# Units 0 to 2 of a chunked-attention and MLP kernel, written out as one list of instructions

## The chip, the cores and the metric

The kernel runs on one core of a Trainium2 chip. The metric is device microseconds of one execution; before the change the median of three runs is 231.96 us (231.26 to 234.47). The core has five engines that run their own instruction queues in order: PE (matmul; PEld is its weight load), DVE, ACT, POOL and SP. Transfers are issued from POOL's queue when they cast, and from SP's or ACT's queue when they don't; all of them share 16 DMA engines.

## What is computed

Attention over chunks of 32 queries, with 16 keys of left context, 8 of right context and 8 memory keys, then a LayerNorm and a two-layer MLP with a residual, over 4 batches of 768 tokens, 8 heads of 64:

```python
for c in range(nc):                                  # nc = 768 // 32
    k_full = concatenate([mem_k, k[:, :, l_start:r_end]], axis=2)
    v_full = concatenate([mem_v, v[:, :, l_start:r_end]], axis=2)
    a = softmax(0.125 * q_c @ k_full.T)
    out[:, :, c_start:c_end] = a @ v_full
x = out.transpose(0, 2, 1, 3).reshape(B, S, 512)
xn = (x - mean(x)) / sqrt(var(x) + 1e-6) * g_ln
y = x + maximum(xn @ w_ch1, 0) @ w_ch2               # 512 -> 2048 -> 512
```

All inputs and the output are 32 bit in memory. The kernel computes in 16 bit with 32-bit sums.

## The kernel before

**Tiles and units.** A tile t (0 to 23) is 128 tokens, six tiles to a batch. A unit u (0 to 11) is two tiles, 256 tokens, the width of an MLP matmul. The attention of a tile runs some units ahead of its MLP.

**Attention of a tile.** `qk_products` (line 305) multiplies the transposed queries QD with the key stream KT, in which the memory keys are repeated in front of every group of 64 keys (`mem_cols`, 189). `row_max` and `less_max` (324, 327) take the row maximum off on DVE, `weights` (337) is the exponential on ACT, `pt` (344) transposes the weights on PE and copies them to PT. `val_products` (355) multiplies them with V, whose rows are [16 left, 16, memory, 24 shared] and the same for the second half of a group; `tokens` (369) divides by the row sums and takes the mean on DVE, `shift` (382) subtracts the mean on POOL or ACT, `turn_x` (410) transposes to x^T on PE and copies it on DVE, `root` (398) computes 1/sqrt(var+eps) on ACT and POOL.

**K, Q and V into place.** An octet is 8 consecutive tokens, 2 KB per head in memory. `load_octets` (108) casts octets of k, q or v into `raw[0]`, `raw[1]` or `raw[2]`, one load for the even heads and one for the odd (`par`). Batch 0 is loaded in two parts and turned by `turn` (208) on PE: 16 small matmuls for two head pairs, then `to_stream` (223) or `to_rows` (232) copies the result out of PSUM. V of batch 0 is turned twice, through the stream VT (the same tile as KT[1]) by `v_products` (278) and `v_copy` (295). Later batches use `mix` (243), a copy that sets two heads side by side, and `turn_mixed` (251), 8 matmuls instead of 16. V of batches 1 to 3 is loaded straight into place, two loads a head (`load_v_head`, 116) and two for the ends; `v_shared` and `v_mem` (140, 144) then copy rows from SBUF to SBUF through SP's queue.

**MLP of a unit.** `up` (447): eight slots s of 8 matmuls with a quarter of w1 (w1c[s // 2]), then a relu. The gain g is multiplied into w1 beforehand, 16 POOL instructions (`scale_w1`, 425). `down` (473) is the plain second layer and serves unit 0; from unit 1 on `down7` (544) does the same with seven products of 8 matmuls in place of eight, with sums of weights (`w2_sum`, 495) and of activations (`r_sum`, 512) made on DVE. `add_to` (533) multiplies by 1/sqrt(var+eps) and adds to x, `store` (539) writes the tile.

**The order.** The program order is each engine's queue order, and the waits between engines follow from the tiles. Units 0 and 1 are written out by hand (603 to 818) with PSUM banks by turns (`slot`, `use`), and with 32 matmuls on zeros as filler (`warm`, 596). From unit 2 (line 884) a plan places attention, loads and sums between the slots `up(u, s)` and the products `down7(u - 1, part)`. Up to line 818 POOL's queue holds, in this order: k and q of octets 0 to 47 and 0 to 31, the identity, v, w1[0], w1[1], the second parts of k, q, v, scaling and w1[2], scaling and w1[3], w2, the other scaling, k and q of batch 1, V of batch 1 head by head.

Of the kernel before, what the change touches and what calls it, by code (L numbers as in the profile page):

```python
# [16 lines left out]
def kernel(  # L17
# [29 lines left out]
    memKT = sb.tile([128, B * 4, 8], FP16, name="memKT")  # L47
    memVT = sb.tile([128, 4, 8], FP16, name="memVT")
# [8 lines left out]
    memk32 = T[1].bitcast(FP32).rearrange("p n (x c) -> p (n x) c", c=64)[0 : B * H, 0:8, :]  # L57
    memv32 = T[1].bitcast(FP32).rearrange("p n (x c) -> p (n x) c", c=64)[0:H, 8:16, :]
    memk16 = T[0].rearrange("p n (x c) -> p (n x) c", c=64)[0 : B * H, 0:8, :]
    memv0 = T[0].rearrange("p n (x c) -> p (n x) c", c=64)[0:H, 8:16, :]  # L60
# [24 lines left out]
    six = one + upb + dnb  # L85
    banks = {"list": six, "turn": 0}
# [4 lines left out]

    def use(*b):
        banks["list"], banks["turn"] = list(b), -1
# [14 lines left out]
    def load_octets(i, half, src, b, lo, n):  # L108

        for par in range(2):  # L110
            nc.gpsimd.dma_start(  # L111
                out=raw[i][half][par : 2 * n : 2],
                in_=dram(src, (b * H + par) * HS + 512 * lo, [[512, n], [2 * HS, 4], [1, 512]]),
            )
# [24 lines left out]

    def v_shared(b, g0, g1):  # L140
        vt = V[b % 2]
        nc.sync.dma_start(out=vt[40:64, g0:g1, :, :], in_=vt[72:96, g0:g1, :, :])

    def v_mem(b, rows=(32, 64), ng=NG):
        src = memv16[:, b, :, :]
        for lo in rows:
            nc.sync.dma_start(
                out=V[b % 2][lo : lo + 8, 0:ng, :, :],
                in_=bass.AP(tensor=src.tensor, offset=src.offset,
                            ap=[list(src.ap[0]), [0, ng], [1, H * VW]]),  # L150
            )
# [12 lines left out]
    def load_mem(dst, src, n):  # L164
        nc.sync.dma_start(out=dst, in_=dram(src, 0, [[512, n], [1, 512]]))
# [9 lines left out]
    def mem_turn(dst, src, n):  # L175

        p = slot()
        half = n // 2
        for m in range(8):
            for par in range(2):  # L180
                nc.tensor.matmul(
                    out=p[64 * par : 64 * par + 64, half * m : half * m + half],
                    lhsT=src[0:n, m, :],
                    rhs=free(identity[0:n, :], 2 * par, [[4, half // 2], [1, 2]]),
                    start=True, stop=True, tile_position=(0, 64 * par),
                )
        nc.vector.tensor_copy(out=dst, in_=free(p, 0, [[1, half], [half, 8]]))

    def mem_cols(dst, src, ends):
        s = list(src.ap[0])  # L190
        nc.vector.tensor_copy(
            out=free(dst, 32, [[KC, 4], [BLK, NG], [1, 8]]),
            in_=bass.AP(tensor=src.tensor, offset=src.offset, ap=[s, [8, 4], [0, NG], [1, 8]]),
        )
        if ends:
            nc.vector.tensor_copy(
                out=free(dst, 0, [[KC, 4], [8, 2], [1, 8]]),
                in_=bass.AP(tensor=src.tensor, offset=src.offset, ap=[s, [8, 4], [0, 2], [1, 8]]),
            )
            nc.vector.tensor_copy(  # L200
                out=free(dst, KC - 8, [[KC, 4], [1, 8]]),
                in_=bass.AP(tensor=src.tensor, offset=src.offset, ap=[s, [8, 4], [1, 8]]),
            )

    def copy_on(engine):
        return nc.scalar.copy if engine == "A" else nc.vector.tensor_copy
# [25 lines left out]
    def to_rows(b, pv, jj, engine, n, oct0, lo=0, hi=None):  # L232
# [7 lines left out]
    mixed = [raw[2][x].rearrange("p j r d -> p (j r d)").rearrange("p (j r c) -> p j r c", j=2, c=128)  # L240
             for x in range(2)]

    def mix(i, half, engine):

        for jj in range(2):
            copy_on(engine)(
                out=mixed[i][0:96, jj].rearrange("p r (x d) -> p x r d", x=2),
                in_=raw[i][half][0:96, 2 * jj : 2 * jj + 2],
            )

    def turn_mixed(i, jj):

        pv = as16(slot())
        for r in range(8):
            nc.tensor.matmul(  # L255
                out=pv[:, 96 * r : 96 * r + 96],
                lhsT=mixed[i][0:96, jj, r, :], rhs=identity[0:96, 0:96],
                is_transpose=True, start=True, stop=True,
            )
        return pv  # L260

# [6 lines left out]
    def turn_k(b, half, jj, engine):  # L268
        to_stream(KT[b % 2], turn(raw[0][half], jj, 48), jj, engine, 48, 48 * half)

    def turn_q(b, half, jj, engine, p=None):
        n, oct0 = (48, 48 * half) if b else ((64, 32) if half else (32, 0))
        to_rows(b, turn(raw[1][half], jj, n, p), jj, engine, n, oct0)

    def turn_v(half, jj, engine):
        to_stream(VT, turn(raw[2][half], jj, 48), jj, engine, 48, 48 * half)

    def v_products(g):

        p = slot()  # L280
# [18 lines left out]

    def v_turn(g, engine):  # L300
        v_copy(g, v_products(g), engine)


# [40 lines left out]
    def pt(t, engine="A"):  # L344
        p = slot()
        pv = as16(p)[:, 0:512]
        for j in range(4):
# [4 lines left out]
            )  # L352
        copy_on(engine)(out=PT[t % 3].rearrange("p j q -> p (j q)"), in_=pv)  # L353

# [27 lines left out]
    def shift(t, engine="P"):  # L382
        x, i = xs[t % 9], t % 3
        if engine == "P":
            nc.gpsimd.tensor_scalar(  # L385
                out=xn[i], in0=x, scalar1=nmean[t % 6], scalar2=1.0, op0=ALU.add, op1=ALU.mult,
            )
        else:
            nc.scalar.activation(
                out=xn[i], in_=x, func=ACTF.Identity, bias=nmean[t % 6], scale=1.0,  # L390
            )
# [6 lines left out]
    def root(t):  # L398
# [4 lines left out]
        )  # L403
        nc.gpsimd.tensor_scalar(  # L404
# [5 lines left out]
    def turn_x(t, p=None):  # L410
        p = slot() if p is None else p
        pv = as16(p)[:, 0:512]
        for dt in range(4):
# [4 lines left out]
            )  # L418
        i = t % 2
        nc.vector.tensor_copy(  # L420
            out=xT[(t // 2) % 3][:, :, 128 * i : 128 * i + 128],
            in_=pv.rearrange("p (d c) -> p d c", d=4),
        )

    def scale_w1(c, dt, engine):
        w = w1c[c][:, dt, :]
        if engine == "A":
            nc.scalar.activation(out=w, in_=w, func=ACTF.Copy, scale=g_col[:, dt : dt + 1])
        elif engine == "V":
            nc.vector.tensor_scalar(  # L430
                out=w, in0=w, scalar1=g_col[:, dt : dt + 1], scalar2=None, op0=ALU.mult,
            )
        else:
            nc.gpsimd.tensor_scalar(
                out=w, in0=w, scalar1=g_col[:, dt : dt + 1], scalar2=1.0,
                op0=ALU.mult, op1=ALU.mult,
            )


# [7 lines left out]
    def up(u, s, engine="A"):  # L447
        p = upb[s % 2]
        for hb in range(2):
            hc = 2 * s + hb  # L450
            for dt in range(4):
# [5 lines left out]
                )  # L457
        relu(rT[u % 2][:, 2 * s : 2 * s + 2, :], p.rearrange("p (h c) -> p h c", h=2), engine)

    def up_half(s, i, p, engine=None):  # L460
# [9 lines left out]
        if engine:  # L470
            relu(rT[0][:, 2 * s : 2 * s + 2, :], p.rearrange("p (h c) -> p h c", h=2), engine)

    def down(u, part):
        i, quarter = divmod(part, 4) if u else (part % 2, part // 2)
        p, t = dnb[i], 2 * u + i
        for hc in range(4 * quarter, 4 * quarter + 4):
            nc.tensor.matmul(  # L477
                out=p, lhsT=rT[u % 2][:, hc, 128 * i : 128 * i + 128],
# [3 lines left out]
        if quarter == 3:  # L482
            x = xs[t % 9]
            nc.vector.scalar_tensor_tensor(
                out=x, in0=p, scalar=rstd[t % 9], in1=x, op0=ALU.mult, op1=ALU.add,
            )
            nc.sync.dma_start(out=out[t // 6, 128 * (t % 6) : 128 * (t % 6) + 128, :], in_=x)
# [56 lines left out]
    def down7(u, part, tail=False):  # L544
        t, s = 2 * u, 2 * u + 1
# [6 lines left out]


        if part == 0:
            product(dnb[0], r_block(u, 0, 0), block(0, 0), False)
            add_to(t, 0, dnb[0])
        elif part == 1:
            product(dnb[1], r_block(u, 0, 1), block(1, 0), False)
            add_to(t, 0, dnb[1])
        elif part == 2:  # L560
            product(dnb[0], RS[1], total(1), True)
            add_to(t, 1, dnb[0])
        elif part == 3:
            product(dnb[1], RS[0], total(0), False)
            add_to(s, 1, dnb[1])
        elif part == 4:
            product(dnb[0], RS[2], total(2), True)
            add_to(s, 1, dnb[0])
            if tail:
                store(s, 256, 512)  # L570
        elif part == 5:
            product(dnb[1], RS[3], block(1, 1), True)
            add_to(t, 1, dnb[1])
            store(t)
        elif part == 6:
            product(dnb[0], r_block(u, 1, 1), total(3), True)
            add_to(s, 0, dnb[0])
# [18 lines left out]
    def warm(n, p=upb[1]):  # L596
# [5 lines left out]

    load_mem(memk32, mem_k, B * H)
    load_mem(memv32, mem_v, H)
    load_octets(0, 0, k, 0, 0, 48)
    load_octets(1, 0, q, 0, 0, 32)
    make_identity(nc, identity)
    load_octets(2, 0, v, 0, 0, 48)
    load_w1(0)
    load_w1(1)  # L610
    load_octets(0, 1, k, 0, 48, 48)
    load_octets(1, 1, q, 0, 32, 64)
    load_octets(2, 1, v, 0, 48, 48)
    nc.gpsimd.memset(last, 1.0)
# [320 lines left out]
```

## Time and profile before

| | |
|---|---|
| median of three runs | 231.96 us (231.26 to 234.47) |
| the profiled execution | 231.75 us, span 230.0 us |
| granted TensorE clock | 1.000 over the span |
| busy: PE, DVE, ACT, POOL | 218.4, 162.1, 124.6, 115.4 us |
| first matmul with w1 (line 464) | 19.30 us |
| first matmuls of unit 3, `up(3, 0)` | 76.61 us |
| scores of tile 0 (line 316) | 9.28 us |

The span runs from the first to the last instruction; some 1.75 us of an execution lie outside it. "Busy" counts an instruction from its start to the modelled end, so that PE can be busy without being dense: 8 matmuls of 256 columns follow each other at 0.87 to 0.88 us in the chain that ended last. A row of the timeline gives the start, the time taken, engine and line, the operation with its output and input, the number of instructions, and in brackets the idle time before it and what ended it.

### The profile page before, as it was taken

The numbers are of one execution on the slowest core, as the hardware profiler recorded it, in microseconds if no ns is written. First come the engines' busy times: TensorE is split into PE (matmuls) and PEld (weight loads), VectorE is DVE, ScalarE is ACT, GpSimd is POOL, SyncE is SP. The second block draws the span as 40 slices with busy tenths as digits, with TensorE's granted clock in tenths as the row PEclk, the third lists the DMA queues.
The fourth block names the chain that finished last, engine by engine and source line by source line (L and its number), as shares of the span: only waits on it lengthen the run. The fifth ranks groups of instructions, "written<-read, shape, count | busy, mean of one in ns | idle before, by whom it ended". The sixth has DMA issues, their size and how long they took to land.

```text
span 230.0 us, 8554 instructions
## 1 busy us (share of the span) xinstructions
PE 218.4 (95%) x3720; PEld 190.0 (83%) x3720; DVE 162.1 (70%) x380; ACT 124.6 (54%) x237; POOL 115.4 (50%) x197
## 2 busy tenths in 40 slices
PE   7979787999999989999999999999999999999993
PEld 3546675886898979989989999999999999899982
DVE  3576654678998996796587796894784875646372
ACT  2244475888552748649645468478447265343310
POOL 7889897589965594913724946513031121220000
PEclk9999999999999999999999999999999999999999
DMA  5999999998999899963881992942102002011022
GB/s 79 188 205 205 214 215 200 187 77 55 61 155 152 149 90 111 138 87 42 149 115 51 119 154 56 106 91 67 48 3 91 3 3 91 3 48 46 1 94 93
DMA packets 43282, 23.25 MB, mean 101 GB/s; under 512 B 29884, under 2 KB 39676, under 8 KB 43172
## 3 DMA queue, kind: packets, MB, share of 16 engines
q0 software_dynamic: 38320, 14.48, 52.9%
q1 hardware_dynamic: 4924, 8.22, 12.8%
q8 instruction: 29, 0.48, 0.8%
q14 instruction: 9, 0.07, 0.1%
HBM read 29.02 MB, written 6.29 MB: 153 GB/s over the span
## 4 chain that ended last, share of the span: by engine, by line
PE 86%; DVE 6%; issue 3%; ACT 2%; POOL 1%; DVEq 0%; POOLq 0%
PE upb L452 34%; PE dnb L528 28%; PE two L362 4%; PE one L255 3%; PE dnb L477 3%; PE one L316 3%; PE one L414 2%; PE two L599 2%; PE one L348 2%; POOL raw L111 1%; DVE sub L328 1%; DVE xs L372 1%; DVE KT L227 1%; DVE nmx L325 1%; ACT rT L443 1%
## 5 line engine op out<-in xcount | busy, mean ns | idle before, releaser
L452 PE MATMUL upb<-xT,w1c 128*128 128x256 f16 x736 | 94.9, 273 | 1.6 <-issue 1.4
L452 PEld LDWEIGHTS <-w1c 128*128 128x128 f16 x736 | 77.8, 114 | 3.6 <-issue 1.5
L443 ACT ACTIVATE rT<-upb 128x512 f16<-128x512 f32 x92 | 53.5, 594 | 37.8 <-PE upb L452 34.9
L535 DVE SCALAR_TENSOR_TENSOR xs<-dnb,rstd,xs 128x256 f32<-128x256 f32 x77 | 37.0, 481 | 27.2 <-PE dnb L528 26.3
L528 PEld LDWEIGHTS <-RS 128*128 128x128 f16 x352 | 33.8, 98 | 3.7 <-issue 0.2
L338 ACT ACTIVATE P<-sub 128x512 f16<-128x512 f32 x24 | 15.2, 634 | 37.1 <-DVE sub L328 36.8
L528 PE MATMUL dnb<-T,RS 128*128 128x256 f16 x264 | 33.9, 273 | 0.0
L385 POOL TENSOR_SCALAR xn<-xs,nmean 128x512 f16<-128x512 f32 x18 | 12.7, 707 | 35.6 <-PE upb L452 20.6
L404 POOL TENSOR_SCALAR veps<-ssq 128x1 f32<-128x1 f32 x24 | 4.9, 204 | 45.9 <-ACT sq L400 45.6
L528 PEld LDWEIGHTS <-rT 128*128 128x128 f16 x264 | 25.2, 98 | 2.5
L528 PE MATMUL dnb<-w2c,rT 128*128 128x256 f16 x176 | 22.7, 272 | 0.0
L522 DVE TENSOR_TENSOR RS<-rT 128x1024 f16<-128x1024 f16 (+2 forms) x23 | 15.2, 663 | 8.9 <-ACT rT L443 8.9
L120 POOL DMA_DIRECT2D V<-in_v_dram x24 | 20.9, 871 | 1.2 <-PE dnb L528 0.7
L400 ACT ACTIVATE sq<-xs,nmean 128x512 f16<-128x512 f32 x24 | 17.3, 721 | 0.1
L372 DVE CUSTOM_DVE_ANT_1 xs<-two,rec 128x512 f32<-128x512 f32 x24 | 16.6, 691 | 0.8
L325 DVE TENSOR_REDUCE nmx<-one 128x8 f32<-128x512 f32 x22 | 15.1, 685 | 1.2 <-PE one L316 1.2
L408 POOL TENSOR_TENSOR rstd<-veps,mhalf 128x1 f32<-128x1 f32 x24 | 14.9, 621 | 2.0
L328 DVE TENSOR_TENSOR sub<-one,nmx 128x512 f32<-128x512 f32 x22 | 15.2, 692 | 0.8
L125 POOL DMA_DIRECT2D V<-in_v_dram x24 | 15.5, 647 | 0.0
L353 ACT COPY PT<-one 128x512 f16<-128x512 f16 x21 | 12.2, 586 | 5.6 <-PE one L348 5.6
L255 PEld LDWEIGHTS <-raw 96*128 96x128 f16 x192 | 10.6, 97 | 2.0 <-issue 0.8
L420 DVE COPY xT<-one 128x512 f16<-128x512 f16 x21 | 8.8, 420 | 4.5 <-PE one L414 4.1
(115 smaller groups left out, 312.2 us busy)
## 6 DMA issues: line engine op xcount, KB each, us to landing
out_dram<-xs SPq DMA_DIRECT2D x23, 256.0 KB, 2.5
raw<-in_k_dram POOLq DMA_DIRECT2D x16, 192.0 KB, 5.8
raw<-in_q_dram POOLq DMA_DIRECT2D x12, 192.0 KB, 6.3
w1c<-in_moe_w_ch_dram POOLq DMA_DIRECT2D x4, 512.0 KB, 8.8
w2c<-in_moe_w_ch_dram POOLq DMA_DIRECT2D x4, 512.0 KB, 12.5
V<-in_v_dram POOLq DMA_DIRECT2D x24, 77.0 KB, 3.7
V<-V SPq DMA_DIRECT2D x3, 360.0 KB
V<-in_v_dram POOLq DMA_DIRECT2D x24, 44.0 KB, 3.4
```

Source lines behind the costliest of these rows:

```text
L120: nc.gpsimd.dma_start(out=V[b % 2][72:128, 0 : NG - 1, h, 0:64], in_=dram(v, base + 16 * D, [[64, 56], [64 * 64, NG - 1], [1, 64]]),)
L125: nc.gpsimd.dma_start(out=V[b % 2][0:32, 1:NG, h, 0:64], in_=dram(v, base + 48 * D, [[64, 32], [64 * 64, NG - 1], [1, 64]]),)
L255: nc.tensor.matmul(out=pv[:, 96 * r : 96 * r + 96], lhsT=mixed[i][0:96, jj, r, :], rhs=identity[0:96, 0:96], is_transpose=True, start=True ...
L325: nc.vector.tensor_reduce(out=nmx[t % 2], in_=scores, axis=AX.X, op=ALU.max)
L328: nc.vector.tensor_tensor(out=sub[t % 2].rearrange("p (c k) -> p c k", c=8), in0=scores, in1=free(nmx[t % 2], 0, [[1, 8], [0, 64]]), op=AL ...
L338: nc.scalar.activation(out=P[t % 3], in_=sub[t % 2], func=ACTF.Exp, scale=0.125)
L372: nc.vector.tensor_tensor_reduce(out=x.rearrange("p (h d) -> p h d", h=H), in0=free(two, 0, [[128, 8], [1, 64]]), in1=free(r, 0, [[1, 8], ...
L400: nc.scalar.activation(out=sq, in_=xs[t % 9], func=ACTF.Square, bias=nmean[t % 6], scale=1.0, accum_out=ssq[i],)
L443: nc.scalar.activation(out=o, in_=i, func=ACTF.Relu)
L452: nc.tensor.matmul(out=p[:, 256 * hb : 256 * hb + 256], lhsT=free(w1c[hc // 4][:, dt, :], hc % 4, [[4, 128]]), rhs=xT[u % 3][:, dt, :], st ...
L528: nc.tensor.matmul(out=p[:, 0:256], lhsT=left[:, n, :], rhs=right(n), start=(n == 0 and not add), stop=(n == 7), skip_group_check=add,)
L535: nc.vector.scalar_tensor_tensor(out=x, in0=p[:, 0:256], scalar=rstd[t % 9], in1=x, op0=ALU.mult, op1=ALU.add,)
```

## The change

Units 0 to 2 become one list in which every step names its PSUM bank and its engine, and the plan starts at unit 3. Helpers are split, so that a matmul group and its copy can stand apart (`v_products` and `v_copy`, `up_products` and `relu_up`, `square` and `root_of`, `down7_products` and `add_to`). The parts:

- The octets 0 to 15 of k, q and v of batch 0 come as 32 bit through SP's queue into xs[6] to xs[8], are cast by ACT and DVE and turned by `first_turn`. The memory rows and the octets 16 and 48 of k and v come through ACT's queue, are cast and turned together (`mem_products`, one copy).
- The rest of batch 0 comes in octets 16 to 47 and 48 to 95, and is turned as later batches are, by `mix_into` and `turn_whole`; three of these copies and two `mix` are on POOL.
- w1 comes after all of batch 0, in the order 3, 2, 0, 1. V of batch 1 comes by groups of 64 keys, two loads a group. Of batch 2, the octets 0 to 47 are loaded and mixed in the list; V of its heads 0 to 3 is moved from unit 2 to unit 4.
- g is multiplied into x^T in the copy out of PSUM (`x_copy`); `scale_w1` is gone. Filler falls from 32 matmuls to 13.

```diff
+    def load_v_group(b, g, part):
+        if part == 0:
+            rows = 56 if g < NG - 1 else 48
+            nc.gpsimd.dma_start(
+                out=V[b % 2][72 : 72 + rows, g, :, 0:64],
+                in_=dram(v, b * H * HS + (64 * g + 16) * D, [[64, rows], [HS, H], [1, 64]]),
+            )
...
+    def load_first(queue, x, src):
+        queue.dma_start(out=xs[6 + x], in_=dram(src, 0, [[512, 16], [HS, H], [1, 512]]))
...
+    def mix_into(m, r, jj, rows, engine):
+        copy_on(engine)(
+            out=m[0:rows, jj].rearrange("p r (x d) -> p x r d", x=2),
+            in_=r[0:rows, 2 * jj : 2 * jj + 2],
+        )
...
+    def x_copy(t, pv):
-        nc.vector.tensor_copy(
+        nc.vector.tensor_tensor(
             out=xT[(t // 2) % 3][:, :, 128 * i : 128 * i + 128],
-            in_=pv.rearrange("p (d c) -> p d c", d=4),
-        )
+            in0=pv.rearrange("p (d c) -> p d c", d=4),
+            in1=free(g_col, 0, [[1, 4], [0, 128]]), op=ALU.mult,
+        )
...
+    load_first(nc.sync, 0, k)
+    load_first(nc.sync, 1, q)
+    load_first(nc.sync, 2, v)
+    load_mem(nc.scalar, 0, mem_k, B * H)
+    load_two(B * H, k)
...
     make_identity(nc, identity)
+    nc.gpsimd.memset(V[0][:, 0:4, :, 64:VW], 1.0)
...
+    warm(7, upb[0])
+    nc.gpsimd.memset(V[0][:, 4:NG, :, 64:VW], 1.0)
...
+    load_octets(1, 0, q, 0, 16, 32, (1,))
...
+    load_octets(0, 0, k, 0, 16, 32, (1,))
...
+    s0 = qk_products(0, upb[1])
...
+    mix_into(whole[0], raw[2][0], 0, 64, "P")
...
+    load_octets(1, 1, q, 0, 48, 48, (1,))
...
+    load_w1(3)
...
+    load_w1(2)
...
+    load_v_group(1, 5, 1)
+    load_w1(0)
...
+    mix_into(whole[2], raw[2][1], 1, 96, "P")
...
+    load_w1(1)
...
+    mix_into(whole[1], raw[0][1], 0, 96, "P")
...
+    shift(1, "P")
...
+    up_products(0, 5, dnb[1])
...
+    load_v_group(1, 3, 0)
...
+    load_v_group(1, 2, 0)
...
+    load_octets(1, 0, q, 1, 0, 48, (1,))
...
+    load_octets(1, 0, q, 1, 0, 48, (0,))
...
+    load_w2(0)
...
+    load_mem_rows(1, B)
+    load_octets(0, 0, k, 1, 0, 48, (0,))
...
+    load_octets(0, 0, k, 1, 0, 48, (1,))
...
+    load_w2(2)
...
     ready_v(1, nc.gpsimd)
...
+    shift(3, "P")
...
+    load_w2(1)
...
+    load_v_group(1, 1, 1)
...
+    load_v_group(1, 8, 1)
...
+    load_v_group(1, 9, 0)
...
+    load_v_group(1, 4, 0)
...
+    load_w2(3)
...
+    load_octets(0, 1, k, 1, 48, 48, (1,))
...
+    load_octets(0, 1, k, 1, 48, 48, (0,))
+    mix(0, 1, "V")
...
+    mix(1, 1, "P")
+    lq10 = turn_whole(mixed[1], 0, 96, dnb[1])
+    to_rows(1, lq10, 0, "A", 48, 48)
+    lk10 = turn_whole(mixed[0], 0, 96, upb[0])
...
+    mix(0, 0, "P")
...
+    root_of(7)
+    relu_up(2, 5, one[1], "A")
+    store(1)
...
+                    at(4, n, load_v_head, b, n // 2, n % 2)
...
-    for u in range(2, NP):
+    for u in range(3, NP):
```

Between w2[3] and the last k of batch 1 the list has, on POOL's queue: V group 1 (part 0), k, group 0 (part 0), q, group 10 (part 1), q, groups 6 and 0 (part 1), group 11 (part 0), k. From the turn `lk10` to the end PE's queue holds 7 `up_products`, 7 `down7_products`, 3 `turn_whole`, 2 `val_products`, 2 `qk_products` and 2 `x_products`. After it, unit 3 begins with `up(3, 0)` and then turns `mixed[0]`, which `mix(0, 0, "P")` has written.

## The prediction

> **What bounds the kernel now.** I read the page first, then tables of busy time by stretch, then the timeline.
>
> ```profile
> span 230.0 us, 8554 instructions
> ...
> PE 218.4 (95%) x3720; PEld 190.0 (83%) x3720; DVE 162.1 (70%) x380; ACT 124.6 (54%) x237; POOL 115.4 (50%) x197
> ...
> PE   7979787999999989999999999999999999999993
> ...
> DMA  5999999998999899963881992942102002011022
> GB/s 79 188 205 205 214 215 200 187 77 55 61 155 152 149 90 111 138 87 42 149 115 51 119 154 56 106 91 67 48 3 91 3 3 91 3 48 46 1 94 93
> ```
>
> One slice is 5.75 us. PE is full from slice 8 on, so only the first 46 us have anything to give; there the DMA engines are at nine tenths in nearly every slice. They move about 205 GB/s with the weights and octets (slices 2 to 7), and 55 and 61 GB/s, as busy, in slices 9 and 10, which are the loads of V. So the start is paced by transfers, the rest by PE.
>
> ```profile
> 10.00:15.00 5.00, 3.51 (x74) 2.00 (x58) 3.40 (x7) 1.49 (x3) 3.23 (x8) 1.00 1.24 204
> ...
> 25.00:30.00 5.00, 3.59 (x104) 3.22 (x97) 3.15 (x6) 2.60 (x6) 4.89 (x8) 1.00 1.14 216
> 30.00:35.00 5.00, 4.33 (x118) 3.63 (x113) 2.98 (x9) 3.73 (x8) 4.94 (x8) 1.00 1.06 213
> 35.00:40.00 5.00, 3.57 (x96) 2.73 (x94) 2.01 (x7) 2.59 (x5) 3.74 (x7) 1.00 1.19 201
> 40.00:45.00 5.00, 4.81 (x54) 4.32 (x55) 3.63 (x8) 3.71 (x9) 2.33 (x4) 1.00 1.37 195
> 45.00:50.00 5.00, 5.00 (x80) 4.34 (x78) 2.92 (x9) 4.88 (x12) 4.26 (x8) 1.00 1.13 99
> ```
>
> The columns are the stretch, its length, busy us of PE, PEld, DVE, ACT and POOL, the granted clock, and DMA. Between 25 and 45 PE is busy 16.3 of 20 us (81%); POOL is nearly full to 35.
>
> ```profile
> 9.28 0.55 PE L316 MATMUL two<-KT,QD 64*32 64x64 f16 x32
> ...
> 10.80 0.58 POOL L111 DMA_DIRECT2D raw<-in_v_dram  x1 [0.74 <-DMA raw<-in_v_dram]
> 13.16 2.70 POOL L434 TENSOR_SCALAR w1c<-w1c,g_col 128x512 f16<-128x512 f16 x4 [0.95 <-DMA w1c<-in_moe_w_ch_dram]
> 25.11 5.36 POOL L434 TENSOR_SCALAR w1c<-w1c,g_col 128x512 f16<-128x512 f16 x8 [0.94 <-DMA w1c<-in_moe_w_ch_dram]
> 38.78 1.14 POOL L111 DMA_DIRECT2D raw<-in_q_dram  x2 [0.83 <-DMA w2c<-in_moe_w_ch_dram]
> 52.33 1.12 POOL L408 TENSOR_TENSOR rstd<-veps,mhalf 128x1 f32<-128x1 f32 x1
> 52.35 1.28 DVE L507 TENSOR_TENSOR T<-w2c 128x1024 f16<-128x1024 f16 x2
> 76.61 1.06 PE L452 MATMUL upb<-xT,w1c 128*128 128x256 f16 x8
> ```
>
> w1[0] is awaited until 13.16 and w1[2] until 25.11, where eight scalings of 0.68 us still stand before PE can have it. At 10.80 POOL's 14th load waits for its 6th, at 38.78 another waits for the eighth before it: eight are in flight at most. Unit 3 starts at 76.61; from there the change leaves the order nearly as it is. So the question is when unit 3 starts in the new list. I call that time T3; the span is 230.0 - 76.6 + T3.
>
> **A formula for landings.** Ahead of and with w1[0] POOL's queue carries 6 loads (4 of 192 KB, 2 of 128 KB) and 512 KB: 1.57 MB, 7.7 us at 205 GB/s. First issue 1.36, so 13.16 - 1.36 - 7.7 = 4.1 us is fixed. Check: through w1[2] it is 3.93 MB, 19.2 us, and 1.36 + 4.1 + 19.2 = 24.7, seen 25.1.
>
> **The change part by part.**
>
> *First octets through SP.* SP's first load (64 KB) was used 1.8 us after its issue at 0.81, POOL's take at least 4.1. Tile 0's scores move from 9.28 to about 7 (k at 3.4, a cast of 0.72, a turn, two copies of 0.5 to 0.6, the same for q). The transfers are 3 x 256 KB uncast, read at 2 x 205 GB/s: 1.9 us, over before POOL's begin. On the path: nothing, since w1 comes later than all this; if w1 were early it would be worth 2 us. ACT issues four loads of its own first, about 0.4 each as on SP (1.6), beside the wait for k. Price: POOL issues its first load after the identity (0.58) and three memsets (0.5 + 0.1 + 0.98): 1.36 + 2.15 = 3.5 instead of 1.36.
>
> *Batch 0 and w1.* Through w1[2]: 6 x 128 KB, 6 x 192 KB, 2 x 512 KB = 3.02 MB, 14.7 us; it lands at 3.5 + 4.1 + 14.7 = 22.3. PE needs it for the first `up`. PE's costs here are distances between starts in the timeline: a turn of 96 columns 0.35 (54.85 to 55.20), scaled to 0.27 for 64; val 0.36 (46.18 to 46.54), scores 0.32 (two in 0.63 from 63.61), v 0.35, pt 0.22, x^T 0.23, 8 matmuls of 256 columns 0.875. Before w1[2] PE has 10.7 us of work (mem 0.5, three first turns 1.2, qk 3 x 0.32, v 6 x 0.35, pt and x 5 x 0.22, val 3 x 0.36, turns 6 x 0.27 and 6 x 0.35), so it waits in any case, and all that is queued behind with it; in the old order the first `up_half` ran at 19.3. POOL must issue w1[2] by 22.3 - 2.6 - 4.1 = 15.6: its queue up to there is 1.4 + 2.1 (start) + 13 x 0.6 + 1.5 (w1) + 0.5 (memset) + 1.4 (one copy) = 14.7, and 0.7 of wait for v before the copy. It just holds.
>
> *scale_w1 away, g on x^T.* 16 x 0.684 = 10.9 us leave POOL. The copy of x^T becomes a two-input one from PSUM: at least the 0.42 of L420, at most the 0.69 of L328, which is the same form; I take 0.69. In the list 8 x 0.27 = 2.2 us of DVE, later 16 x 0.27 = 4.3; DVE is 70% busy and PE finds x^T four steps later, so nothing. Without that cover 4.3 us.
>
> *POOL's copies.* 1024 columns; no such row. Bounds: the 0.98 memset of 1024 below, twice 0.684 (512 columns, L434) = 1.37 above; I take 1.37, the same operand traffic. 3 single + 2 double = 7 x 1.37 = 9.6 us.
>
> *V by groups.* 24 loads of 0.55 to 0.65 (L131, L135) replace 16 of 0.87 and 0.65 plus two ends: 14.4 against 13.4 us of POOL. The packets are the same 128 bytes, at 58 GB/s: a part 0 (57 KB) takes 0.99 us, a part 1 (33 KB) 0.57.
>
> *The transfers after w1[2]*, back to back (192 KB: 0.96, 512 KB: 2.56): w1[0] 25.5, w1[1] 28.0, two V parts and q 31.9, w2[0] 34.5, k 36.4, w2[2] 39.0, w2[1] 41.5, four V parts 44.6, w2[3] 47.2, then six V parts and four octet loads (8.5): the last k of batch 1 lands at 55.7. Its `mix` on DVE (0.77) ends at 56.5, and PE's turn `lk10` waits for it.
>
> *PE against this.* From 22.3 to `lk10` PE has 30.3 us of work (17 ups x 0.875, 8 quarters of down x 0.865, 5 turns, 3 val, 5 pt, 4 x, 5 qk, 6 v): dense it would be there at 52.6, so transfers decide, with 3.9 us of waiting. From `lk10` on: 7 x 0.875 + 7 x 0.875 + 3 x 0.35 + 2 x 0.36 + 2 x 0.32 + 2 x 0.23 = 15.1. T3 = 56.5 + 15.1 = 71.6.
>
> *Other engines up to T3.* POOL: 48 V and octet loads 28.8, weights and rows 6.0, copies 9.6, 4 shifts 2.8, 8 roots 6.4, memsets 6.9 = 60.5 us. ACT: 18 relus 10.7, 10 exponentials 6.3, 8 squares 7.4, 16 copies to streams and rows 13.0, 9 of V 5.5, 4 mixes 4.2, 4 shifts 2.9, 5 of weights 2.9, first octets and memory 5.3 = 58.2. DVE: 20 row operations 13.8, 8 `tokens` 9.0, 8 x^T 5.5, weight sums 5.1, 6 relus 4.1, sums and adds 7.6, streams and rows 4.6, V and weights 2.5, mixes 4.5, the start 3.6 = 60.3. All fit under 71.6, none with much room. POOL's last long step, `mix(0, 0, "P")`, is awaited by PE 0.9 us into unit 3.
>
> *From unit 3.* Four heads of V of batch 2 move into unit 4: 8 x 0.75 = 6 us on POOL in a unit of 15 us, where it is half idle; their SBUF copies have 7 steps before tile 12 needs them. A shift behind them is 1 to 2 us late, five steps early. Zero; if that cover fails, about 2 us.
>
> Sum: T3 from 76.6 to 71.6, -5.0. The profiled execution, 231.75, becomes 226.7; it lies 0.2 under the median of 231.96.
>
> **The rivals.**
>
> *PE dense.* If transfers run faster than my rates, PE is dense after 22.3: 22.3 + 30.3 + 15.1 = 67.7, time 222.8. For it: slices of 214 and 215. Against: the check on w1[2] came out 0.4 late, not early.
>
> *As loose as before.* If engines wait for each other as between 25 and 45 (81%), the 30.3 us take 37.2; T3 = 74.6, time 229.8. For it: ACT, DVE and POOL are each as loaded as PE.
>
> *The clock.* Filler falls from 32 to 13, and up to 22.3 PE works under 60% of the time. The trace keeps clock 1.00 at 70% (10 to 15 us) and after a gap of 1.4 us; less is not shown. At half clock 10.7 + 1.4 us double and the first `up` comes at 4.4 + 24.2 = 28.6; T3 between 74.0 and 77.9, time about 231. The Trainium skill, "TensorE: Matmul & The Clock Gate", section "What's actually happening", takes the clock away only after an idle window of about 3.4 us; by that nothing happens here, since no such gap is in the list.
>
> *POOL becomes the bound (slower).* At 52.33 the power op took 1.12 where it takes 0.56 alone, beside a 16-bit sum on DVE. If POOL's copies double likewise (+9.6) and it idles 14 us, as it did in the first 75 us before, it ends at 60.5 + 9.6 + 14 = 84.1; the mix is through 0.8 earlier, PE meets it 0.9 into unit 3: T3 82.4, time 237.6. It decides from 12 us of copies and waits above the sum. Against: rows of L434 stay within 682 to 698 ns beside DVE. The Trainium skill, "GPSIMD Engine Reference", section "Key points", says that POOL shares its SBUF ports with DVE; it speaks for this case.
>
> *SP's loads land no sooner.* Then tile 0 is 2 us later, PE at 69.7 if dense, still under the transfers: 226.7 to 227.7.
>
> **How the numbers follow.** Forecast 45% (own range 224.9 to 228.6), PE dense 15%, loose 20%, clock 6%, POOL 10%, SP 4%. Without POOL's case and most of the clock's: 222.5 to 231.0. A measurement tells about 2% from no change, 227.3 to 236.6. Faster: 15 + two thirds of 45 + 2 of loose + 3 of SP = 50%. Slower: POOL's 10, 1 of the clock = 11%. Same: 39%.
>
> **What would show it.** Right: w1[2] awaited until 22 to 23; w2[1] near 41.5; DVE's mix of k waiting for a load near 55; `up(3, 0)` near 71.6; clock 1.00. Wrong: POOL's copies above 2 us, loads issued late with DMA slices under nine tenths before 50, PE waiting at the first turn of unit 3, a clock below 1 before 25 us.

## The result, and the profile after

The changed kernel takes 241.56 us (median of 4 runs, 240.70 to 242.24) against 233.03 of the kernel before beside it (4 runs): the ratio is 1.037, with an interval of 1.028 to 1.046. It is slower; forecast were 226.7 us. The profiled execution took 240.70 us, with a span of 238.9.

From the page of the changed kernel, the busy times and the slices (5.97 us each):

```profile
span 238.9 us, 8348 instructions
...
PE 217.9 (91%) x3605; PEld 192.1 (80%) x3605; DVE 168.3 (70%) x377; ACT 131.6 (55%) x257; POOL 115.2 (48%) x198
...
PE   5297699999999999999459999999999999999994
...
PEclk9679589999999999999958999999999999999999
DMA  6999989999796992976932298693201102001022
```

Counted from 0, PE is full from slice 5 on, but for slices 19 and 20, where nothing was expected; ahead of that it has holes in slices 1, 3 and 4. Around both stretches the granted clock falls too. By stretches (the columns are those of the prediction's table):

```profile
5.00:10.00 5.00, 0.00 (x0) 0.00 (x0) 0.25 (x1) 0.41 (x1) 3.02 (x6) 0.76 1.13 179
10.00:15.00 5.00, 4.55 (x102) 2.80 (x102) 3.14 (x13) 2.94 (x11) 3.22 (x5) 0.56 1.23 183
...
20.00:25.00 5.00, 3.33 (x109) 2.44 (x110) 4.25 (x8) 5.00 (x9) 1.46 (x2) 0.96 1.29 201
25.00:30.00 5.00, 4.12 (x75) 3.86 (x74) 2.58 (x7) 2.72 (x6) 2.52 (x4) 0.50 0.91 144
...
110.00:130.00 20.00, 14.07 (x229) 11.80 (x227) 8.81 (x19) 6.21 (x12) 6.11 (x11) 0.83 0.67 109
```

PE does nothing from 5 to 10 us, and 14.07 us in the 20 from 110 to 130. The timeline names what it waited for:

```profile
0.80 0.40 ACTq L174 DMA_DIRECT2D T<-in_mem_k_dram  x1
1.24 1.22 ACTq L179 DMA_DIRECT2D T<-in_k_dram  x1
2.50 0.30 ACTq L174 DMA_DIRECT2D T<-in_mem_v_dram  x1
2.84 0.63 ACTq L179 DMA_DIRECT2D T<-in_v_dram  x1
...
2.94 0.76 POOL L105 DMA_DIRECT2D raw<-in_q_dram  x1
...
9.75 0.42 DVE L662 CAST T<-T 72x512 f16<-72x512 f32 x1 [8.48 <-DMA T<-in_v_dram]
...
10.23 0.62 PE L201 MATMUL one<-identity,T 72*64 72x36 f16 x16 [5.87 <-DVE T L662]
...
12.74 0.29 PE L360 MATMUL upb<-KT,QD 64*32 64x64 f16 x8
13.20 0.51 PE L360 MATMUL upb<-KT,QD 64*32 64x64 f16 x24 [0.17 <-DVE g_col L678]
...
25.88 0.24 PE L411 MATMUL two<-V,PT 64*32 64x65 f16 x3 [2.08 <-issue]
...
30.75 1.39 PE L495 MATMUL dnb<-xT,w1c 128*128 128x256 f16 x8
...
77.42 1.04 PE L495 MATMUL upb<-xT,w1c 128*128 128x256 f16 x8
78.29 0.51 PE L312 MATMUL one<-identity,raw 96*128 96x96 f16 x8
...
110.12 0.76 SPq L151 DMA_DIRECT2D V<-V  x1
...
110.93 2.70 SPq L156 DMA_DIRECT2D V<-memv  x2
...
119.16 0.19 PE L411 MATMUL two<-V,PT 64*32 64x65 f16 x1 [3.31 <-DMA V<-memv]
...
121.97 0.62 PE L411 MATMUL two<-V,PT 64*32 64x65 f16 x31 [2.62 <-DMA V<-memv]
```

Two places, then. **The start:** DVE's cast of the memory rows and octets 16 and 48 waits until 9.75 for the last of ACT's four small loads, issued at 2.84. The turns of the first octets and so the scores of tile 0 stand behind it, the first `up` (L495) starts at 30.75 where 22.3 was forecast, and unit 3 at 77.42 instead of 71.6 (76.61 before). **Unit 4:** SP's two copies of the memory rows into V (`v_mem`) are issued at 110.93, right behind the copy of the shared rows (`V<-V`), and PE waits for them twice, 5.9 us in all. In the kernel before they went out at 100.44:

```profile
100.44 2.34 SPq L147 DMA_DIRECT2D V<-memv  x2
```

From unit 3 to the end the changed kernel needs 238.9 - 77.4 = 161.5 us, the one before 230.0 - 76.6 = 153.4.

### The profile page after: what moved, and what is told of

Its sections match the earlier page's. It is cut to its first block, busy times and chain, and to the rows that moved or that the text cites. A ratio compares the mean times of both kernels' runs of the same rounds, so it can differ in the third digit from the quotient of the medians.

```text
span 238.9 us, 8348 instructions
## 1 busy us (share of the span) xinstructions
PE 217.9 (91%) x3605; PEld 192.1 (80%) x3605; DVE 168.3 (70%) x377; ACT 131.6 (55%) x257; POOL 115.2 (48%) x198
## 4 chain that ended last, share of the span: by engine, by line
PE 80%; DMA 7%; DVE 6%; ACT 3%; issue 2%; ACTq 1%; DVEq 0%
PE upb L495 27%; PE dnb L572 26%; DMA V<-memv 4%; PE two L411 4%; PE dnb L495 4%; PE one L312 3%; DMA T<-in_v_dram 3%; PE one L495 3%; PE one L360 2%; PE one L467 2%; PE one L391 2%; PE dnb L521 1%; PE upb L312 1%; PE one L521 1%; DVE sub L372 1%
## 5 line engine op out<-in xcount | busy, mean ns | idle before, releaser
L495 PEld LDWEIGHTS <-w1c 128*128 128x128 f16 x768 | 81.9, 115 | 3.2 <-issue 0.5
L495 PE MATMUL upb<-xT,w1c 128*128 128x256 f16 x608 | 79.8, 276 | 0.0
L487 ACT ACTIVATE rT<-upb 128x512 f16<-128x512 f32 x75 | 43.7, 595 | 31.7 <-PE upb L495 31.7
L434 POOL TENSOR_SCALAR xn<-xs,nmean 128x512 f16<-128x512 f32 x20 | 14.5, 726 | 46.4 <-DVE nmean L427 26.9
L411 PE MATMUL two<-V,PT 64*32 64x65 f16 x768 | 11.0, 195 | 8.5 <-DMA V<-memv 5.9
L411 PEld LDWEIGHTS <-PT 64*32 64x32 f16 x768 | 7.8, 95 | 13.3 <-issue 9.3
L476 DVE TENSOR_TENSOR xT<-one,g_col 128x512 f16<-128x512 f16 x19 | 13.1, 687 | 5.1 <-PE one L467 3.3
L114 POOL DMA_DIRECT2D V<-in_v_dram x16 | 13.5, 844 | 0.1
L399 ACT COPY PT<-one 128x512 f16<-128x512 f16 x17 | 9.9, 584 | 4.3 <-PE one L391 4.3
L369 DVE TENSOR_REDUCE nmx<-one 128x8 f32<-128x512 f32 x16 | 11.0, 686 | 1.3 <-PE one L360 1.3
L495 PE MATMUL dnb<-xT,w1c 128*128 128x256 f16 x88 | 11.5, 279 | 0.0
```

The source lines that it names most:

```text
L114: nc.gpsimd.dma_start(out=V[b % 2][72:128, 0 : NG - 1, h, 0:64], in_=dram(v, base + 16 * D, [[64, 56], [64 * 64, NG - 1], [1, 64]]),)
L411: nc.tensor.matmul(out=two[col : col + 32, 128 * h : 128 * h + 65], lhsT=PT[t % 3][rows, 2 * (h // 4) + h % 2, q0 : q0 + 32], rhs=V[b % 2] ...
L434: nc.gpsimd.tensor_scalar(out=xn[i], in0=x, scalar1=m, scalar2=1.0, op0=ALU.add, op1=ALU.mult,)
L487: nc.scalar.activation(out=o, in_=i, func=ACTF.Relu)
L495: nc.tensor.matmul(out=p[:, 256 * hb : 256 * hb + 256], lhsT=free(w1c[hc // 4][:, dt, :], hc % 4, [[4, 128]]), rhs=xT[u % 3][:, dt, :], st ...
```

## The experiments

My explanation: `v_mem` alone costs the 8.1 us after unit 3, and ACT's loads land late since they go out when POOL's are already under way, and hold the first `up`. Its rivals: the steps that the prediction priced at nothing (g on x^T, V by groups, the moved heads) cost those 8 us; the load of two octets is slow by its form; the lower clock is the cost of the start.

All numbers of the runs stand in one table, from each kernel's profiled execution: the start of the cast of the memory rows, of the first `up` and of unit 3, and the span less unit 3's start; the last column is the median of 4 to 10 executions. The runs were made at several times; the kernel before, measured beside each, had medians of 232.2 to 233.0 us, so that a difference between two medians of the table is uncertain by up to 0.8 us.

| | cast | first up | unit 3 | from there on | median us |
|---|---|---|---|---|---|
| changed kernel | 9.75 | 30.75 | 77.42 | 161.5 | 241.56 |
| e1_vmem_early | 9.61 | 30.65 | 77.71 | 153.1 | 233.65 |
| e2_two_8row | 7.37 | 29.58 | 77.00 | 161.8 | 238.75 |
| e3_two_first | 10.55 | 31.18 | 78.23 | 161.7 | 242.18 |
| e4_fill | 9.55 | 29.39 | 76.81 | 162.1 | 240.18 |
| e6_rows_early | 5.38 | 26.59 | 74.71 | 152.8 | 229.40 |
| e7_rows_fill | 5.54 | 26.44 | 73.25 | 153.7 | 229.09 |
| e8_late_fill | 9.68 | 30.28 | 76.55 | 154.7 | 233.67 |
| e10_loads_away | 8.46 | 30.30 | 77.37 | 157.2 | 235.52 |
| e11_pool_hold | 7.53 | 27.78 | 74.76 | 153.6 | 231.24 |
| e12_rows_early_alone | 5.73 | 26.90 | 73.91 | 162.6 | 237.21 |
| e13_half_fill | 5.85 | 26.78 | 73.11 | 154.0 | 228.81 |

### The copies of the memory rows

**e1_vmem_early**

```diff
-        at(u0 + 1, late, v_mem, b)
+        at(u0 + 1, 0 if b == 2 else 6, v_mem, b)
```

> The copies of the memory rows into V of batch 2 (v_mem) go from step 13 to step 0 of unit 4; all else as in the changed kernel. Theory 1: the 6 us in which PE stands still near 116 to 122 us, and the half clock after them, come from these copies being issued at 110.9 us. Then PE finds them done, the clock keeps 1.00 between 110 and 130 us, and the time falls by 7 to 8 us, to about 234. Rival: the SBUF copies of the shared rows (v_shared), issued just before them at 110.1, or the last loads of V are late too; then PE still waits there, for V from another transfer, and the gain is under 4 us.

Measured: 233.65 us, ratio 1.006 (1.003 to 1.009). The stretch from 110 to 130:

```profile
110.00:130.00 20.00, 20.00 (x322) 18.66 (x320) 14.55 (x31) 11.47 (x22) 10.79 (x18) 1.00 0.74 126
```

PE is busy all 20 us and the clock stays at 1.00. It waits for no copy into V: the shared rows, the rival of the expectation, are in time (issued at 110.34, used at 116.07).

```profile
110.34 0.79 SPq L151 DMA_DIRECT2D V<-V  x1
...
116.07 0.42 PE L411 MATMUL two<-V,PT 64*32 64x65 f16 x32
```

From unit 3 on it is 153.1 us, the 153.4 of before. So one line costs 8 us, and g on x^T, V by groups and the moved heads cost nothing from there on.

**e10_loads_away**: is it the late issue, or POOL's loads beside the copies?

```diff
-                at(w, 1, load_octets, 0, half, k, b, 48 * half, 48)
-                at(w, 3, load_octets, 1, half, q, b, 48 * half, 48)
-                at(w, 12, mix, 0, half, "V")
+                late = w == 5
+                at(w, 5 if late else 1, load_octets, 0, half, k, b, 48 * half, 48)
+                at(w, 7 if late else 3, load_octets, 1, half, q, b, 48 * half, 48)
+                at(w, 15 if w == 5 else 12, mix, 0, half, "V")
...
-                    step = (0, 2, 4, 12, 13, 14, 15, 16)[n]
+                    step = ((9, 10, 11) if w == 5 else (0, 2, 4))[n] if n < 3 else n + 9
```

> The changed kernel, with the two SBUF copies of the memory rows still at the late step (issued near 111 us), but POOL's five loads of unit 5 (three of V, k and q of batch 3, issued at 110 to 113) put behind the first values of the unit, and the mix of that k from step 12 to step 15. If the two copies landed 8 and 11 us after their issue because POOL's packets run beside them, PE's wait for V<-memv falls from 5.9 us to at most 1.5 and the time from 241.6 to about 234.5 (up to 2 us more if the mix waits for k). If they take that long by themselves, the wait stays above 4 us and the time above 239.

Measured: 235.52 us, ratio 1.014 (1.009 to 1.018). PE's waits, in the timeline:

```profile
110.76 2.35 SPq L156 DMA_DIRECT2D V<-memv  x2
...
116.60 0.19 PE L411 MATMUL two<-V,PT 64*32 64x65 f16 x1 [0.84 <-DMA V<-memv]
118.66 0.47 PE L411 MATMUL two<-V,PT 64*32 64x65 f16 x31 [1.88 <-DMA V<-memv]
```

The wait is 2.7 us, between the two expectations, so neither was whole. The first copy is there 5.8 us after issue (116.60 - 110.76) instead of 8.2 (119.16 - 110.93), the second 2.1 after that instead of 2.8. PE wants them 5.0 us after issue (116.60 - 0.84 - 110.76). Issued this late, the copies come too late even without POOL's loads; with them beside the copies the wait more than doubles, and with the half clock that follows it they are 4 of the 8 us by the profiled executions (161.5 against 157.2) and 6 by the medians. Both copies also stand right behind `V<-V`, 360 KB on the same queue; no run shows how much of the 5.8 us is that.

### Why the first rows landed late

**e2_two_8row**

```diff
-        nc.scalar.dma_start(
-            out=mem32[lo : lo + 2 * H],
-            in_=dram(src, 16 * 512, [[32 * 512, 2], [HS, H], [1, 512]]),
-        )
+        for n in range(2):
+            nc.scalar.dma_start(
+                out=mem32[lo + n * H : lo + n * H + H],
+                in_=dram(src, (16 + 32 * n) * 512, [[HS, H], [1, 512]]),
+            )
```

> Each load of the octets 16 and 48 (16 rows, outermost count 2 on the memory side) is split into two loads of 8 rows (outermost count 8), on ACT's queue as before. Theory 1: the load of v's octets lands at 9.7 us because it runs on few DMA engines and shares them with POOL's loads; split, the memory rows are cast at about 5.5 to 6.5 us instead of 9.75, the granted clock stays at 1.00 up to 15 us, and the time falls by 4 to 6 us. Rival 1 (late on ACT's queue): two more issues of 0.3 to 0.6 us make it later still; no gain or a loss of 1 us. Rival 2 (the engines are simply full with the uncast 768 KB and POOL's loads): the cast stays at 9 to 10 us, no gain.

Measured: 238.75 us, ratio 1.026 (1.018 to 1.033), an interval that overlaps that of the changed kernel; the cast at 7.37, 2.4 us sooner. So the form seems to have a part. The Trainium skill, "DMA: Bandwidth & Descriptors", section "Why a DMA increments its semaphore by 16 and not by 1", has such a load run on the largest number of DMA engines, up to 16, that divides the size of the slowest dimension on both sides; by that the load of two octets would use two engines, its halves eight. No run here shows the engines of a load; the sign agrees. The size is less sure: e10_loads_away has the first 30 us of the changed kernel unchanged, and its cast came at 8.46, so 1.3 us of the 2.4 may be scatter.

**e3_two_first**

```diff
+    load_two(B * H + 3 * H, v)
+    load_two(B * H, k)
     load_mem(nc.scalar, 0, mem_k, B * H)
-    load_two(B * H, k)
     load_mem(nc.scalar, B * H + 2 * H, mem_v, H)
-    load_two(B * H + 3 * H, v)
```

> The two loads of octets 16 and 48 stand first on ACT's queue, unsplit, and the memory rows behind them. Theory 1 (few engines, shared with POOL's loads): issued before POOL's first load they are through early; the cast starts at 5 to 6 us, time 4 to 6 us less. Rival 1 (late issue): the same gain; it differs from theory 1 in the run with split loads, where it expects none. Rival 2 (engines full): the cast stays at 9 to 10 us, no gain.

Measured: 242.18 us, ratio 1.041 (1.033 to 1.048). The cast:

```profile
10.55 0.42 DVE L662 CAST T<-T 72x512 f16<-72x512 f32 x1 [9.28 <-DMA T<-in_mem_v_dram]
```

Now the wait is for `in_mem_v`, 16 KB in 8 rows, a load of the other form, and it ends later still. So the form alone isn't it: in both kernels the load that ACT issues last, beside or behind POOL's first (2.94), is the late one.

**e11_pool_hold** (with e1's edit): three more memsets ahead of POOL's first load.

```diff
     warm(7, upb[0])
+    nc.gpsimd.memset(V[0][:, 4:NG, :, 64:VW], 1.0)
+    nc.gpsimd.memset(V[0][:, 4:NG, :, 64:VW], 1.0)
+    nc.gpsimd.memset(V[0][:, 4:NG, :, 64:VW], 1.0)
     nc.gpsimd.memset(V[0][:, 4:NG, :, 64:VW], 1.0)
```

> The changed kernel with the copies of the memory rows of batch 2 early (233.7 us) and three more memsets of 0.94 us ahead of POOL's first load, which so goes out near 5.8 instead of 2.94. ACT's four loads are as in the changed kernel, in number, size, order and time of issue. If the last of them landed at 9.7 because POOL's packets were ahead of it, the cast of the memory rows comes at 5.5 to 6.5, and since everything of POOL's is 2.8 us later the first up is near 28 and the time near 231. If two of them are slow by their own form or queue, the cast stays above 8 us and the time is 234 to 236.

Measured: 231.24 us, ratio 0.992 (0.988 to 0.996).

```profile
2.84 0.63 ACTq L179 DMA_DIRECT2D T<-in_v_dram  x1
...
5.96 0.77 POOL L105 DMA_DIRECT2D raw<-in_q_dram  x1
...
7.53 0.59 DVE L665 CAST T<-T 72x512 f16<-72x512 f32 x1 [6.25 <-DMA T<-in_v_dram]
```

POOL starts 3 us later, and the kernel becomes 2.4 us faster than e1. The time is the one expected (231); the cast at 7.53 is between the two expectations. With POOL silent until 5.96, ACT's loads still share the engines with SP's 768 KB. So late landing seems to have two parts of some 2 us: the company of POOL's packets (e1's 9.61 to 7.53), and what is left when they come later (7.53 to the 5.38 of e6; the form, or SP's loads). The scatter of 1.3 us applies to both, and how the second part divides wasn't tried.

**e6_rows_early** (with e1's edit): the rows go out ahead of q and v, half from ACT, half from SP, in loads of 8 rows (`load_two` as in e2, with the queue as an argument).

```diff
     load_first(nc.sync, 0, k)
-    load_first(nc.sync, 1, q)
-    load_first(nc.sync, 2, v)
     load_mem(nc.scalar, 0, mem_k, B * H)
-    load_two(B * H, k)
-    load_mem(nc.scalar, B * H + 2 * H, mem_v, H)
-    load_two(B * H + 3 * H, v)
+    load_two(nc.scalar, B * H, k)
+    load_mem(nc.sync, B * H + 2 * H, mem_v, H)
+    load_two(nc.sync, B * H + 3 * H, v)
+    load_first(nc.sync, 1, q)
+    load_first(nc.sync, 2, v)
```

> On top of the early v_mem: the memory rows and octets 16 and 48 are issued before the first octets of q and v, half on ACT's queue, half on SP's, in loads of 8 rows, so that all of them are issued by about 2.6 us, ahead of POOL's first load at 2.9. Theory 1 (late issue on a hardware queue behind POOL's loads): the memory rows are cast at 5 to 6 us, not 9.6; tile 0's scores at about 8; but the clock is lost again between 15 and 30 us, since PE's work there is as thin as before, so unit 3 starts at 74 to 76 instead of 77.7 and the time is 230 to 232. Rival (few engines on each such load): the cast stays after 7 us and nothing is gained over the early v_mem alone, 233.7.

Measured: 229.40 us, ratio 0.983 (0.977 to 0.989): faster than the kernel before. The cast comes at 5.38 and unit 3 at 74.71.

**e12_rows_early_alone**: the same without e1's edit.

> The memory rows and octets 16 and 48 issued ahead of q and v, half from ACT and half from SP, as in e6_rows_early, but the SBUF copies of the memory rows of batch 2 left late. If the two costs stand apart, the 4.3 us of the first come off alone: 237.3, unit 3 near 74.7, PE's wait for V<-memv still 4 to 6 us. If the wait for V<-memv is only there because the start is late, the time is near 229.4.

Measured: 237.21 us, ratio 1.020 (1.016 to 1.025); PE waits 6.8 us for `V<-memv`. The two costs add: 241.6 - 237.2 = 4.4 for the rows, 237.2 - 229.4 = 7.8 for the copies.

### The clock and the filler

**e4_fill** (the changed kernel with 22 more fillers in the first gap)

```diff
-    warm(7, upb[0])
+    warm(29, upb[0])
```

> 22 more matmuls on zeros stand behind the first seven, about as long as PE's wait from 4.4 to 10.2 us; nothing else changes. Theory 1: the wait itself costs some 5 us, and the lost clock that follows another 2 to 3; with the filler the memory rows are still cast at 9.75, the clock stays at 1.00 from 5 to 22 us, and the time falls by 1 to 3 us. Rival: the clock costs nothing since transfers pace the start anyway; no change within 0.5 us.

Measured: 240.18 us, ratio 1.033 (1.027 to 1.039), not clear of the changed kernel's 1.037 (1.028 to 1.046).

```profile
15.00:18.00 3.00, 2.29 (x81) 1.82 (x78) 2.89 (x8) 3.00 (x7) 3.00 (x5) 1.00 1.17 161
18.00:20.00 2.00, 1.67 (x56) 1.35 (x53) 1.97 (x7) 2.00 (x6) 1.96 (x3) 0.57 1.21 189
20.00:25.00 5.00, 4.44 (x108) 3.44 (x102) 3.48 (x8) 4.05 (x8) 1.22 (x2) 0.50 1.24 190
```

The clock is kept through the gap and falls to one half at about 18.3 (0.57 from 18 to 20), though PE is busy three quarters of the time there and has no gap above 0.83 us. The Trainium skill, "TensorE: Matmul & The Clock Gate", section "What's actually happening", ties the half clock to an idle window of about 3.4 us. In the changed kernel the clock fell within PE's wait of 5.87 us (0.76 from 5 to 10), which agrees; here it came without such a window, and the measurement decides. ACT is full in the first two rows (3.00 of 3, 2.00 of 2).

**e8_late_fill** (e1 with 26 more fillers at twelve places of the list before the first `up`, and 22 in the gap) and **e7_rows_fill** (e6 with the same 26, and 4 in the gap). Such lines are added, here two:

```diff
+    warm(3, one[1])
     p0 = pt_products(0, one[1])
...
+    warm(2, upb[0])
     s1 = qk_products(1, upb[0])
```

> Early v_mem, loads as in the changed kernel, with the same filler as in the run before and 22 matmuls in the first gap. Theory 2: clock 1.00 throughout; what is left is the late cast at 9.6 us alone; unit 3 at 75 to 76, time 230 to 231.5, so that late rows cost about 3 us and the clock about 2.5. Rival (clock costs nothing): 233.7 as with the early v_mem alone.

> As the run with the rows early, with 30 more matmuls on zeros in twelve places up to 28 us. Theory 2 (the clock is kept by how much PE works, not by the absence of long gaps): clock 1.00 throughout, unit 3 starts at 72 to 73.5 us, time 226.5 to 228.5. Rival 1 (the clock costs nothing, ACT and DVE pace the start): no change against the run without filler. Rival 2: the filler delays PE where it had no room; slower by up to 2 us.

Measured: e8 233.67 us, ratio 1.004 (1.001 to 1.008), clock 0.997; e7 229.09 us, ratio 0.983 (0.978 to 0.988), clock 0.998. Both have the time of the same kernel without filler (233.65, 229.40). So the rival came true in both: a kept clock bought by filler is worth nothing here. That does not say that the lost clock is free, since the filler itself takes PE's time.

**e13_half_fill** therefore cut 28 of e7's fillers to half their columns.

```diff
-    def warm(n, p):
+    def warm(n, p, c=512):
...
-    warm(3, one[1])
+    warm(3, one[1], 256)
```

> The kernel of e7_rows_fill with 28 of its filler matmuls, those after the scores of tile 0, cut from 512 to 256 columns: some 3 us less of filler between 9 and 26.5 us, where the chain of e7_rows_fill is PE without a gap up to 20.5. If the clock stays at 1.00 and PE with its filler paced that stretch, the first up comes at 24 to 25 instead of 26.4 and the time is 226.5 to 227.5, near the forecast. If ACT, DVE or the landing of w1[2] pace it, the first up stays at 26 or later and the time at 229. If the clock falls to one half as in e6_rows_early, both stay as well, and the clock's row tells these two apart.

Measured: 228.81 us, ratio 0.987 (0.983 to 0.991); the first `up` at 26.78.

```profile
19.75 0.39 PE L468 MATMUL one<-identity,xn 128*128 128x128 f16 x4
...
20.38 0.20 PE L412 MATMUL two<-V,PT 64*32 64x65 f16 x2
22.07 0.42 PE L412 MATMUL two<-V,PT 64*32 64x65 f16 x30 [1.49 <-issue]
```

Up to 19.75 PE is 1.3 us ahead of e7 (x^T of tile 0 at 21.06 there). Then a group of matmuls stops in its middle for 1.49 us with no releaser, the clock is at one half from 23.0 to 26.4 (0.75 from 22 to 24, 0.50 to 26, 0.89 to 28), and nothing is left. Neither expectation is met: what the stretch would take at full clock without the stop stays open.

The traces of all twelve kernels divide the end of this stretch, though. From x^T of tile 0 (19.75 here, 22.92 in the changed kernel) to the first `up` it takes:

| | us | clock | ACT busy |
|---|---|---|---|
| e3, e7, e8, e12 | 5.28 to 5.39 | 0.95 to 1.00 | 5.05 to 5.39 |
| e2, e4, e6, e10 | 6.21 to 6.53 | 0.50 to 0.57 | 5.40 to 5.72 |
| with a stop of PE: changed kernel, e1, e11, e13 | 6.20 to 7.83 | 0.61 to 0.76 | 5.28 to 5.78 |

So the half clock costs about 1 us there, and a stop with the lower clock behind it 1 to 2.5; at full clock ACT is all but full, which points to ACT as what paces it then. These are single executions, and the 13.2 to 15.9 us from the cast to x^T don't divide in this way.

### One part alone

**e9_g_alone**: the kernel before with g at x^T and without `scale_w1`.

```diff
-        nc.vector.tensor_copy(
+        nc.vector.tensor_tensor(
             out=xT[(t // 2) % 3][:, :, 128 * i : 128 * i + 128],
-            in_=pv.rearrange("p (d c) -> p d c", d=4),
+            in0=pv.rearrange("p (d c) -> p d c", d=4),
+            in1=free(g_col, 0, [[1, 4], [0, 128]]), op=ALU.mult,
...
     for c in range(2):
-        for dt in range(4):
-            scale_w1(c, dt, "P")
         load_w1(2 + c)
```

> The kernel before, with one part of the change alone: g is multiplied into x^T in the copy out of PSUM, and the 16 scalings of w1 on POOL are gone. Theory: the second half of w1 is usable at 25 instead of 30 us and POOL issues the loads of batch 1 some 5 to 10 us earlier; the wider copies cost DVE 6.5 us that are covered. PE's gaps between 25 and 40 us shrink by 1 to 3 us: time 229 to 231. Rival (PE's gaps there come from the order of the list and from code loading, not from w1): no change within 0.5 us.

Measured: 232.15 us, ratio 0.998 (0.995 to 1.001), unit 3 at 76.66 (76.61 before): the rival's time, and not the 229 to 231 of the theory. From its list of waits up to 77 us:

```profile
POOL raw L111 <- DMA w1c<-in_moe_w_ch_dram: 3.9, 2, 2.2
...
POOL w1c L154 <- DMA w1c<-in_moe_w_ch_dram: 3.0, 2, 1.9
```

Eleven us of work leave POOL, and POOL waits for w1 6.9 us where it waited 1.9. Between 10 and 25 us the transfers run at 206 GB/s, before at 205. That fits the prediction's view that in the old order transfers set the pace of the start; the rival's own reason (the order of the list and code loading) wasn't tried apart from it.

## Why the prediction was wrong

The miss is 240.7 - 226.7 = 14.0 us: 5.8 up to unit 3 (77.4 for 71.6), 8.1 after it (161.5 for 153.4).

**The step that failed most** is "From unit 3": "their SBUF copies have 7 steps before tile 12 needs them. [...] Zero; if that cover fails, about 2 us." I counted steps, and never asked how long a copy takes: 7 steps were 4.9 us here (110.93 to 115.85), and the copies were there 8.2 and 11 us after the first one's issue (5.8 and 7.9 without POOL's loads beside them). The trace of before could have warned: its SP issued them at 100.44, 10.5 us sooner, and POOL issued no load between 97.5 and 109.68. And the failed cover cost 8 us, four times my price, since PE, after waiting for 6 us, went on at half clock (0.83 over the stretch).

**"First octets through SP ... On the path: nothing".** I costed the *issues* of ACT's four loads (1.6 us; they took 2.7, 0.80 to 3.47) and not their *landing*. The 1.8 us that SP's load of 64 KB took when the queues were empty doesn't hold for loads issued beside POOL's first: the last took 6.9 (2.84 to 9.75). Scores came from 12.7 to 13.7 for "about 7". This was worth 4.2 to 4.4 us, as e1 against e6 and e12 against the changed kernel show.

**"It lands at 3.5 + 4.1 + 14.7 = 22.3. PE needs it for the first `up`"** (w1[2]). The first `up` doesn't wait for w1[2] in any of these runs: in the changed kernel it was issued at 15.8 and landed 8.6 us later, at 24.4 (2.1 later than forecast), and the first `up` is at 30.75; in e6 it landed at 23.1 (14.3 + 8.8), and the first `up` is at 26.59. It follows the cast of the memory rows, by 19.8 to 22.2 us in all twelve kernels of the table. I had added PE's own work before it, 10.7 us, as if it ran dense; it is the attention of tile 1, step by step through PE, DVE, ACT and POOL, with ACT at 5.00 of 5 between 20 and 25. So even with the rows early it starts at 26.4 to 26.9. Which engine sets these 21 us isn't settled as a whole: kept clock, half clock, and more or less filler gave nearly the same sum. In the last 5 to 8 of them the half clock costs about 1 us, a stop of PE with it 1 to 2.5, and at full clock ACT is all but full (table above).

**"transfers decide, with 3.9 us of waiting".** From the first `up` to unit 3 it takes 46.3 to 48.1 us in every run, for 45.4 of work: PE is dense there, since everything starts later and the transfers have landed. 49.3 were forecast, so 2.6 of the 8.4 us came back. "PE dense" was the right picture of that stretch, and not of what stands ahead of it.

**Right or harmless.** The copy of x^T is 0.69 us, as taken, and costs nothing. POOL's copies are 1.03 us single (1.37 taken, bounds 0.98 and 1.37), 2.5 for a pair beside DVE; POOL never became the bound: PE's first turn of unit 3 at 78.29 waits for nothing. V by groups costs nothing. POOL issued w1[2] at 15.8 where 15.6 was needed. The clock did fall, which the prediction gave 6%: it counted on a list without long gaps, and the wait of 5.87 us for the memory rows is one. Its cost is about 1 us in the stretch where it can be read; that rival had 6.3 us up to the first `up` (28.6 for 22.3).

With both mishaps mended the change does gain: 229.4 us, a ratio of 0.983 (0.977 to 0.989), where 226.7 of 231.96, 0.977, was forecast. Its unit 3 starts at 74.71, 3.1 us behind the forecast. That is the number of the rival "As loose as before" (74.6, 229.8), but by luck: the first `up` is 4.3 us late, and from there PE is nearly dense (48.1 us for 45.4 of work). None of the rivals reached the 240.7 us of the change itself.

## What to carry to other kernels

Price a transfer that is moved by its time from issue to landing in the company that it will have, not by its issue or by the steps in between. Loads on which the first work of the kernel stands go out before any other queue has traffic. And where the first use of a weight is forecast from its landing, work out the chain through all engines that leads to the other operand as well: here it was 21 us for 11 us of matmuls.

## What the runs showed of the hardware

- Copies of 120 KB from SBUF to SBUF onto 8 partitions, right behind one of 360 KB on SP's queue, took 5.8 us from issue to use with POOL's queue quiet, and 8.2 with its loads of k, q and V beside them; a 16 KB load took 6.9 us (issued at 3.6, used at 10.5, e3) where 64 KB took 1.8 on idle queues.
- PE's clock fell to one half at three quarters busy, without a gap above 0.83 us (e4), and soon after a stop of 1.49 us (e13); in the kernel before a stop of 1.4 us left it at 1.00.
- PE stopped for 1.0 to 2.1 us inside a group of matmuls, with no releaser in the trace, six times before 45 us (until 25.88 in the changed kernel, 25.77 in e1, 23.51 in e11, 22.07 in e13, 26.47 and 38.54 in the kernel before). Each time a 16 KB packet of the queue of kind "instruction" started 0.4 to 1.3 us ahead of the stop (at 23.37 for that of the changed kernel). Other such packets passed without a stop (28.26 there), and what causes the stops wasn't tried.
